# Gated mix of linear and softmax attention, one core: maxima moved to the front, and attention in cycles of two steps

## The chip, the cores and the metric

The kernel runs on one core of a Trainium2 chip. The metric is the device time of one execution in microseconds; three executions of the kernel before took 1025.98, 1026.76 and 1027.21 us (median 1026.76). A core has a matrix engine (PE, with its weight loads listed apart as PEld), a vector engine (DVE), an activation engine (ACT), a general engine (POOL), and a queue that issues DMA (SP). Each runs its own list of instructions in order, and waits on semaphores for the others.

## What is computed

The input x has 2048 rows of 448. Two attention layers with 16 heads of 28 work on it, and a gate mixes them:

```
A: q, k, v = heads(x @ A_wqkv);  pq = q @ w_phi;  pk = k @ w_phi      (per head)
   phi(p) = [softmax(p), softmax(-p)]
   o = phi_q (phi_k^T v) / (phi_q sum(phi_k) + 1e-6);   a = o @ A_wo
B: q, k, v = heads(x @ B_wqkv)
   p = softmax(q k^T * 28**-0.5);   o = p v;             b = o @ B_wo
g = sigmoid(sum(x * gate_w));   out = g a + (1 - g) b
```

## The kernel before, in words

**Order.** PE, DVE, ACT and POOL run in the order in which the Python code emits their instructions; for SP a scheduler chooses the order. So the place of a call in the source is its place in each engine's list.

**Front, about 0 to 331 us.** First come the projections of q and k of layer B (`proj_qk`, `first_units`), kept in DRAM. Then a loop over `i` (line 698) makes layer A. For its first 16 turns, `t` from 0 to 15, each turn multiplies one block of 128 rows by the folded k weights (`pk`, by `tok_major`, 11 passes, line 726) and by the v weights (`value_a`, 11 passes, line 483). Each second turn has a `proj_qk` as well, and `kv_add`. From `pk`, `features1` and `features2` make the softmax features: a copy on ACT, two reductions on DVE, two subtractions on POOL, an exponential on ACT, a sum and a reciprocal on DVE, a product on POOL. The later turns make the numerators of layer A and its output (`out_a`, tile `poa`, 12 passes) and the values of layer B (`value_b`, tile `pvb`, 11 passes). A last loop (line 878) makes `pvb` 8 to 15.

**Maxima.** The softmax of layer B subtracts the exact maximum of each row, found ahead of the scores. That work is cut into 256 units of four matmuls with 28 rows of weights each (row tiles of the array, which run at the same time). Units are made in two ways:

- In the front, `mx_unit` (line 259) writes four banks of PSUM as two tiles, `pmb` and `pmd`. ACT takes the relu of `pmd` (128x1024, line 288), two DVE operations (line 290) combine it with `pmb`. Only four banks are there for it, so the `pmd` matmuls of a unit wait for the DVE work of the unit before. `NF` = 28 units are made so: four among the last projections, one at the start of each even turn, two at turns 16 and 17, then one or two a turn from turn 24 on (lines 666, 704, 741, 787), until 28 are used up. The calls at lines 876 and 882 then find nothing left to do. Keys and queries of a unit are loaded from DRAM ahead of it (`pair_load`, `pair_query`), with two subtractions on POOL.
- In the attention loop, `mx_visit` (line 305) makes one unit in four single banks, `pm`: ACT takes the relu of one (line 326), DVE reduces the other three (lines 330 and 333), each fourth visit a further one (line 336). So 228 visits are left.

`mx_reduce` gathers the maxima of 512 rows and 4 heads (one `gq` of 16), and `load_nm` puts them, negated, into the stack of queries before the scores of that `gq` begin.

**Attention loop, about 331 to 1010 us, line 1091.** There are 16 `gq` of 16 steps, 256 steps. A step `s` makes four scores (`st`, one bank each, 128 rows of weights, line 840) and their four exponentials on ACT (`p`, line 858), the values of step `s - 1` (`pv`, column tiles of 32, line 974, eight matmuls), and a visit as long as there are visits (steps 1 to 228). So PE runs four `st`, eight `pv`, four `pm`, four `st`, and so on. Eight banks of PSUM are shared out: one for `pv`, seven for scores and visits. The lists `free`, `used` and `held` (lines 853 to 864 and 911 to 916) hand out the seven in turn; a bank can be written again when its reader, ACT or DVE, is done with it.

At the end of a `gq`, `finish` copies `pv` out on DVE (`f1`, line 399), sends the denominators through DRAM (`f2`, three steps later), multiplies on POOL (`f3`, eight steps later) and splits the product in two on POOL (`f4`). Near the end, `project` (tile `pob`, 11 passes, lines 984 and 109) makes the output of 128 rows at steps 230 to 233, 239 to 242 and 250 to 253 (`PROJ`); `load_out` fetches what it needs at the steps of `OUTS`.

Of the kernel before, what the change touches and what calls it, by code (L numbers as in the profile page):

```python
# [8 lines left out]
F32 = mybir.dt.float32  # L9
F32R = mybir.dt.float32r  # L10
# [7 lines left out]
P = 128  # L18
S = 2048
D = 448  # L20
# [3 lines left out]
NG = 4  # L24
# [2 lines left out]
SCALE = DH ** -0.5  # L27
EPS = 1e-6
NU = NG * NQ * 16
NF = 28  # L30
LOWEST = -3.0e38
OUTS = (200, 234, 243, 206)
PROJ = (230, 239, 250)


def f32(ap):
# [4 lines left out]
def gated_mix_kernel(ctx, tc, xT, wqkB, wvB, wvA, wkAT, wqAT, phi, woA, woB,  # L41
# [352 lines left out]

    def normalize1(pool, pn, nm, n):

        oU = pool.tile([P, n, 512], F32, tag="oU", name=f"oU{nm}", bufs=1 + n)
        for i in range(n):
            (nc.scalar.copy if n == 2 else nc.vector.tensor_copy)(oU[:, i, :], pn[i])
        den = pool.tile([P, n, 16], F32, tag="den", name=f"den{nm}", bufs=2)  # L400
        for i in range(n):
            nc.sync.dma_start(den[:, i, :], oU[DH:P:32, i, :])
        return oU, den

    def normalize2(pool, oU, den, nm, n, eps):

        if eps:
            nc.vector.tensor_scalar_add(den, den, EPS)
        nc.vector.reciprocal(den, den)
        rd = dr.tile([4, n * 512], F32, tag=f"rd{n}", name=f"rd{nm}", bufs=2)  # L410
        rs = pool.tile([P, n, 512], F32, tag="rs", name=f"rs{nm}", bufs=2)
        for k in range(n):
            nc.sync.dma_start(rd[:, k * 512:(k + 1) * 512], den[:, k, :])
        nc.sync.dma_start(rs.rearrange("p n q -> p (n q)"),
                          rd.unsqueeze(1).to_broadcast([4, 32, n * 512]))
        return oU, rs
# [6 lines left out]
    def normalize4(pool, oU, nm, n):  # L423

        oTn = []
        for k in range(n):
            oT = pool.tile([P, 2, 512], F32R, tag="oT", name=f"oT{nm}_{k}", bufs=2 * n)
            (nc.scalar.copy if n == 2 else nc.gpsimd.tensor_copy)(oT[:, 0, :], oU[:, k, :])
            nc.gpsimd.tensor_sub(oT[:, 1, :], oU[:, k, :], f32(oT[:, 0, :]))
            oTn.append(oT)  # L430
        return oTn
# [402 lines left out]
    def scores(s, i):  # L834

        gq, kt = divmod(s, NT)
        g, qb = divmod(gq, NQ)

        def score(j, st):
            nc.tensor.matmul(st, kst_of[(g, kt // 4)][:, j, (kt % 4) * P:(kt % 4 + 1) * P],  # L840
                             qst_of[gq][:, j, :], start=True, stop=True)
# [9 lines left out]
        sts = []  # L851
        for j in (2 * i, 2 * i + 1):
            used.append(free.pop(0))
            sts.append(bank(used[-1], f"st{s}_{j}"))
            score(j, sts[-1])
        for st in sts:
            p = late_p.tile([P, 512], F32, tag="p", name=f"p{s}_{len(pts.get(s, []))}", bufs=8)
            nc.scalar.activation(p, st, AF.Exp, scale=SCALE)  # L858
            pts.setdefault(s, []).append(p)
        if i == 1:  # L860
            a, m = used[:], held[:]
            free.extend([a[0], m[0], a[1], m[1], a[2], a[3], m[2]] if m else a)
            used.clear()
            held.clear()

    qst = [stack("qst0", False)]
    kst = [stack(f"kst{i}", True) for i in range(5)]
# [27 lines left out]

    free, used, held = list(range(7)), [], []
    spare = []

    def bank(i, nm):
# [15 lines left out]

    def spare_open():
        free.extend(held)
        held.clear()  # L920
# [90 lines left out]
    def finish(gq, s):  # L1011

        st = {}
        g, qb = divmod(gq, NQ)
        last = gq == NG * NQ - 1

        def f1():
            st["n"] = normalize1(late_p, [pv_of[gq]], f"b{gq}", 1)

        def f2():  # L1020
            st["n"] = normalize2(late_p, *st["n"], f"b{gq}", 1, False)

        def f3():
            st["n"] = normalize3(*st["n"], 1)

        def f4():
            st["o"], = normalize4(late_p, st["n"], f"b{gq}", 1)
            if g < NG - 1:
                for j in range(4):
                    r = (4 * g + j) * DH  # L1030
                    nc.sync.dma_start(o_d[r:r + DH, :, qb * 512:(qb + 1) * 512],
                                      f32(st["o"][32 * j:32 * j + DH]))

        if last:
            finish_last(gq)
            return
        f1()
        late.setdefault(s + 3, []).append(f2)
        late.setdefault(s + 8, []).append(f3)
        late.setdefault(s + 9, []).append(lambda: acts.append(f4))  # L1040
        if g == NG - 1:
            for tl in range(4):
                mids[PROJ[qb] + tl] = lambda tl=tl: project(qb, st["o"], tl)

    def finish_last(gq):

        oU = late_p.tile([P, 512], F32, tag="oU", name="oUlast", bufs=2)
        nc.vector.tensor_copy(oU, pv_of[gq])
        tail_fill(4)
        pd = bank(free.pop(0), "pd")  # L1050
# [5 lines left out]
        oT = late_p.tile([P, 2, 512], F32R, tag="oT", name="oTlast", bufs=2)  # L1056
        rw = late_p.tile([P, 16, 32], F32, tag="rs", name="rw", bufs=2)
        nc.vector.tensor_copy(rw, rc.unsqueeze(2).to_broadcast([P, 16, 32]))
        tail_fill(4)
        pr = bank(free.pop(0), "pr")  # L1060
# [27 lines left out]
            take_lows(),  # L1088
            b == 2 and nc.gpsimd.tensor_copy(woB_s[96:, 1, 2, :], woB_s[:32, 0, 2, :]))))

    for s in range(NS + 16):
        take_acts()
        if s < NS:
            gq, kt = divmod(s, NT)
            g, qb = divmod(gq, NQ)
            if s in (0, 3):
                load_k(0, 2 + s // 3)
# [6 lines left out]
            if s in OUTS:  # L1104
                load_out(OUTS.index(s))
            if g == NG - 1 and kt == 12:
                load_acc(qb)
            if s:
                scores(s, 0)
                scores(s, 1)  # L1110
        if s == NS:
            tail_open()
            tail_fill(3)
        if 0 < s <= NS:
            values(s - 1)
            if s % NT == 0:
                finish(s // NT - 1, s)
        if s:
            mx_visit()
        if mxs["f"] == len(flats):  # L1120
            mx_fin()
        if s in mids:
            mids.pop(s)()
# [4 lines left out]
        for fn in late.pop(s, []):  # L1128
            fn()


# [66 lines left out]
```

## Time and profile before

| | us |
|---|---|
| runs (three) | 1025.98, 1026.76, 1027.21 |
| the profiled execution, its own time | 1026.18 |
| span of its instructions on the core | 1024.4 |
| PE clock granted | 1.00 throughout |
| front, up to the first visits | 0 to 331 |
| 228 steps with a visit | 331 to 926 |
| 28 steps without one, with 12 projections | 926 to 1010 |
| last normalization and output | 1010 to 1024.4 |

The views of the profile used below are these. The page has busy times by engine and the chain of work that ended last. The windows give the busy time of each engine in a stretch. The timeline lists instructions in order of time, alike neighbours merged: start, length, engine, line, operation, tiles, shape, count, and in brackets the idle time before and what ended it. The chain of waits lists the pieces of the chain: start, length, what. Matmul lengths include the pipeline's latency, so what a matmul costs is read from the start of one to the start of the next.

### The profile page before, as it was taken

To read this page: it belongs to the slowest core of one execution; us is meant where nothing else is said; L and a number is where in the kernel's file an instruction comes from. 1 tells how busy PE (TensorE), PEld (TensorE's weight loads), DVE (VectorE), ACT (ScalarE), POOL (GpSimd) and SP (SyncE) were. 2 spreads that over 40 slices of the span, in tenths; PEclk is the share of its full clock that TensorE was granted. 3 is DMA by queue.
4 is the path that set the end of the run, shared out by engine and by line. 5 is a ranking of instruction groups with operands and counts; after the bars stand their busy time and mean duration, and the time that the engine had idled before them with its cause. 6 is when DMAs were issued, how large, how long until landed. Compare 5 with 4: busy or idle time off the path is not lost.

```text
span 1024.4 us, 17747 instructions
## 1 busy us (share of the span) xinstructions
PE 1014.4 (99%) x6344; PEld 560.0 (55%) x6344; DVE 685.9 (67%) x1335; ACT 811.1 (79%) x1534; POOL 244.8 (24%) x213
## 2 busy tenths in 40 slices
PE   8999999999999999999999999999999999999998
PEld 6878888878798333333333333333333333335555
DVE  5465556997610778887878878788888788882102
ACT  5354444777734999999999999999999999996672
POOL 1235456687428003301011010010120101101010
PEclk9999999999999999999999999999999999999999
DMA  8873110132337412324422223432222436312341
GB/s 295 294 245 105 51 43 22 41 90 97 97 115 153 92 47 66 82 64 107 98 53 70 72 69 84 96 70 58 70 75 64 116 95 170 85 37 78 105 126 54
DMA packets 63857, 98.65 MB, mean 96 GB/s; under 512 B 17896, under 2 KB 24664, under 8 KB 63768
## 3 DMA queue, kind: packets, MB, share of 16 engines
q1 hardware_dynamic: 63768, 97.51, 35.1%
q8 instruction: 50, 0.82, 0.4%
q14 instruction: 39, 0.32, 0.1%
HBM read 69.31 MB, written 27.78 MB: 95 GB/s over the span
## 4 chain that ended last, share of the span: by engine, by line
PE 94%; DMA 2%; DVE 2%; SPq 0%; issue 0%; ACT 0%; POOL 0%; POOLq 0%; DVEq 0%; ACTq 0%
PE st L840 28%; PE pv L974 24%; PE pm L322 10%; PE pqk L109 5%; PE poa L109 4%; PE pk L109 4%; PE pva L109 4%; PE pq L109 3%; PE pob L109 3%; PE pvb L109 2%; PE pvb L127 2%; PE pn L533 1%; PE pft L521 1%; PE pmb L285 1%; PE pkv L476 1%; PE poL L1008 1%
## 5 line engine op out<-in xcount | busy, mean ns | idle before, releaser
L858 ACT ACTIVATE p<-st 128x512 f32<-128x512 f32 x1020 | 525.8, 610 | 28.9 <-PE st L840 28.1
L333 DVE TENSOR_REDUCE part<-pm 128x1 f32<-128x512 f32 x513 | 327.6, 685 | 139.2 <-PE pm L322 132.3
L840 PE MATMUL st<-qst,kst 128*128 128x512 f32 x1024 | 316.4, 431 | 0.1
L974 PE MATMUL pv<-p,vb 128*32 128x512 f32 x2048 | 272.7, 605 | 0.0
L840 PEld LDWEIGHTS st<-qst,kst 128*128 128x128 f32 x1024 | 173.0, 187 | 130.5 <-issue 66.3
L322 PEld LDWEIGHTS pm<-kc,qc 28*128 28x128 f32 x912 | 43.6, 181 | 191.2 <-ACT p L858 182.8
L326 ACT ACTIVATE rl<-pm 128x512 f32<-128x512 f32 x228 | 136.5, 599 | 11.6
L420 POOL TENSOR_TENSOR oUb<-oUb,rsb 128x512 f32<-128x512 f32 x15 | 19.3, 1287 | 513.4 <-DMA rsb<-rdb 296.4
L330 DVE CUSTOM_DVE_ANT_0 rl<-pm,rl 128x512 f32<-128x512 f32 x171 | 116.3, 680 | 0.0
L322 PE MATMUL pm<-kc,qc 28*128 28x512 f32 x912 | 115.2, 495 | 0.0
L974 PEld LDWEIGHTS pv<-p,vb 128*32 128x32 f32 x2048 | 40.3, 108 | 65.4 <-issue 61.0
L109 PE MATMUL pqk<-XH,wB 128*128 128x512 f32 x192 | 59.6, 398 | 2.5 <-DVE ev L573 2.5
L985 DVE SCALAR_TENSOR_TENSOR acc<-pob,gate,acc 128x448 f32<-128x448 f32 x12 | 8.2, 683 | 67.9 <-PE pob L109 67.9
L572 ACT CAST ev<-pqk 128x512 fp32r<-128x512 f32 x28 | 15.9, 589 | 37.3 <-PE pqk L109 32.8
L109 PE MATMUL poa<-woA_s,oTa 128*128 128x448 f32 x192 | 42.8, 372 | 0.0
L290 DVE CUSTOM_DVE_ANT_0 rl<-pmb,rl 128x512 f32<-128x512 f32 x56 | 36.2, 684 | 8.8 <-ACT rl L288 8.8
L109 PEld LDWEIGHTS pqk<-XH,wB 128*128 128x128 f32 x192 | 35.3, 188 | 11.4 <-DVE ev L573 3.0
L573 DVE TENSOR_TENSOR ev<-pqk,ev 128x512 fp32r<-128x512 f32 x28 | 18.9, 689 | 29.7 <-ACT ev L572 29.5
L336 DVE TENSOR_REDUCE part<-rl 128x1 f32<-128x512 f32 x57 | 38.5, 675 | 0.0
L109 PEld LDWEIGHTS poa<-woA_s,oTa 128*128 128x128 f32 x192 | 35.4, 188 | 5.0 <-issue 1.8
L109 PE MATMUL pk<-wkA_s,XH 128*128 128x448 f32 x128 | 37.4, 374 | 0.0
L109 PE MATMUL pq<-wqA_s,XH 128*128 128x448 f32 x128 | 37.3, 374 | 0.0
(155 smaller groups left out, 1132.7 us busy)
## 6 DMA issues: line engine op xcount, KB each, us to landing
qkd<-ev SPq DMA_DIRECT2D x28, 512.0 KB
qst<-qkd SPq DMA_DIRECT2D x64, 224.0 KB
kst<-qkd SPq DMA_DIRECT2D x64, 224.0 KB
od<-oTb SPq DMA_DIRECT2D x48, 112.0 KB
rsa<-rda SPq DMA_DIRECT2D x8, 512.0 KB
rsb<-rdb SPq DMA_DIRECT2D x15, 256.0 KB
kc<-qkd SPq DMA_DIRECT2D x64, 56.0 KB
gad<-ga SPq DMA_DIRECT2D x16, 224.0 KB
```

The lines of the kernel that those rows point to most:

```text
L109: nc.tensor.matmul(dst, l, r, start=i == 0, stop=i == len(todo) - 1)
L127: nc.tensor.matmul(dst[:, :n], l, r, start=i == 0, stop=i == len(todo) - 1, skip_group_check=True)
L290: nc.vector.tensor_tensor_reduce(rl[:, i, :], pb[:, i, :], rl[:, i, :], 1.0, LOWEST, ALU.add, ALU.max, part[:, col + i:col + i + 1])
L322: nc.tensor.matmul(pm[j], mxs[("qc", gq)][js, qt * P:(qt + 1) * P], mxs[("kc", g, kb)][js, :], start=True, stop=True, tile_position=(32 * ...
L326: nc.scalar.activation(rl, pm[kb], AF.Relu if kb < 3 else AF.Copy)
L330: nc.vector.tensor_tensor_reduce(r, pm[j], r, 1.0, LOWEST, ALU.add, ALU.max, part[:, col + j:col + j + 1])
L333: nc.vector.tensor_reduce(part[:, col + j:col + j + 1], pm[j], AX.X, ALU.max)
L336: mxs["fin"].append(lambda: nc.vector.tensor_reduce(part[:, col + 3:col + 4], rl, AX.X, ALU.max))
L420: (nc.gpsimd if n == 1 else nc.vector).tensor_mul(oU, oU, rs)
L840: nc.tensor.matmul(st, kst_of[(g, kt // 4)][:, j, (kt % 4) * P:(kt % 4 + 1) * P], qst_of[gq][:, j, :], start=True, stop=True)
L858: nc.scalar.activation(p, st, AF.Exp, scale=SCALE)
L974: nc.tensor.matmul(pv[32 * j:32 * j + 32, :], vb[kt // 8][:, kt % 8, 4 * g + j, :], pt[j], start=kt == 0, stop=kt == NT - 1, tile_position ...
```

## The change

The attention loop takes two steps as one cycle in steps 1 to 104 and 233 to 254: eight scores, then the values of two steps (16 matmuls), then at most one visit. Steps 105 to 232 stay single, with a visit each. So 180 visits are made in the loop, 52 of them in the 52 cycles. The other 76 units are made in the front: 24 more inside the first 16 turns, at even distances within the passes of `pk` and `value_a` (`tick`, `pace`), 12 more among `poa` and `pvb` (the calls that stood there already), and 12 around and inside `pvb` 8 to 14 (the calls of lines 876 and 882). In the program, the numbers of the additional units are 5 to 7, 9 to 11 and so on up to 33 to 35, then 52 to 63, then 64 to 75.

Banks are handed out in a fixed order (`cycle_banks`): in a cycle of two steps, scores 0 to 4 take three banks of `late3` and two of `visit`, scores 5 and 7 take the banks of scores 0 and 1 again, and score 6 the third bank of `visit`. In single steps the order comes to that of before. Twelve `p` tiles are kept instead of 8; to make room, `oU`, `rs` and `oT` of the loop have one buffer instead of two. The steps of loads and projections near the end are moved, and `f3`, `f4` come a step earlier.

```
-NF = 28
+NF = 76
+LAST = 232
-OUTS = (200, 234, 243, 206)
-PROJ = (230, 239, 250)
+OUTS = (200, 238, 246, 206)
+PROJ = (234, 242, 250)
...
-        oU = pool.tile([P, n, 512], F32, tag="oU", name=f"oU{nm}", bufs=1 + n)
+        oU = pool.tile([P, n, 512], F32, tag="oU", name=f"oU{nm}", bufs=2 * n - 1)
...
-        rs = pool.tile([P, n, 512], F32, tag="rs", name=f"rs{nm}", bufs=2)
+        rs = pool.tile([P, n, 512], F32, tag="rs", name=f"rs{nm}", bufs=n)
...
-            oT = pool.tile([P, 2, 512], F32R, tag="oT", name=f"oT{nm}_{k}", bufs=2 * n)
+            oT = pool.tile([P, 2, 512], F32R, tag="oT", name=f"oT{nm}_{k}", bufs=3 * n - 2)
...
-        tok_major(pv, t, wvA_s, 450)
+        tok_major(pv, t, wvA_s, 450, tick)
...
+    pace = {}
+
+    def tick(_):
+
+        if pace["at"] and pace["n"] >= pace["at"][0]:
+            pace["at"].pop(0)
+            mx_unit()
+        pace["n"] += 1
...
         if t < NT and t % 2 == 0:
             mx_unit()
+            passes = (55 if t < NT - 4 else 44) + (4 if t >= 4 else 0)
+            pace["n"], pace["at"] = 4 if t >= 4 else 0, [k * passes // 4 for k in (1, 2, 3)]
...
-            tok_major(pk, t, wkA_s, D)
+            tok_major(pk, t, wkA_s, D, tick)
...
+        sts = [bank(b, f"st{s}_{j}") for j, b in enumerate(i)]
+        for j in range(4):
+            score(j, sts[j])
+        pts[s] = [late_p.tile([P, 512], F32, tag="p", name=f"p{s}_{j}", bufs=12) for j in range(4)]
+        for j in range(4):
+            nc.scalar.activation(pts[s][j], sts[j], AF.Exp, scale=SCALE)
...
+    late3, visit = [0, 1, 2], [3, 4, 5, 6]
+    free = []
...
+    def cycle_banks(n):
+
+        x, y = late3[:], visit[:]
+        if spare:
+            b = [(free.append(free.pop(0)), free[-1])[1] for _ in range(4 * n)]
+        elif n == 1:
+            b = x + y[:1]
+            late3[:], visit[:] = [b[2], b[3], y[3]], [b[0], y[1], b[1], y[2]]
+        else:
+            b = x + y[:2] + [x[0], y[2], x[1]]
+            late3[:], visit[:] = b[5:], [y[3], b[2], b[3], b[4]]
+        return b
+
     def mx_banks(f, first):
-        b = [free.pop(0) for _ in range(4)]
-        free.append(b[0])
-        held.extend(b[1:])
         order = [first] + sorted({0, 1, 2, 3} - {first}, key=lambda j: j == first - 1)
-        return [bank(b[order.index(j)], f"pm{f}_{j}") for j in range(4)]
+        return [bank(visit[order.index(j)], f"pm{f}_{j}") for j in range(4)]
...
-        late.setdefault(s + 8, []).append(f3)
-        late.setdefault(s + 9, []).append(lambda: acts.append(f4))
+        late.setdefault(s + 7, []).append(f3)
+        late.setdefault(s + 8, []).append(lambda: acts.append(f4))
...
-    for s in range(NS + 16):
+    first = 2 * (LAST - len(flats) // 4)
+    s = 0
+    while s < NS + 16:
+        n = 2 if 0 < s <= first or LAST < s < NS - 1 else 1
+        steps = range(s, s + n)
+        s += n
         take_acts()
...
+        if 0 < steps[0] < NS:
+            b = cycle_banks(n)
+            for i, t in enumerate(steps):
+                scores(t, b[4 * i:4 * i + 4])
...
+        for t in steps:
+            if 0 < t <= NS:
+                values(t - 1)
+                if t % NT == 0:
+                    finish(t // NT - 1, t)
+        if steps[0]:
             mx_visit()
...
```

More of the change, by code (lines that the diff above doesn't have):

```diff
@@ L850, in scores @@
             return
[L851 to L864, printed above, removed]
+        sts = [bank(b, f"st{s}_{j}") for j, b in enumerate(i)]
[4 more added lines that the diff above has]
+            nc.scalar.activation(pts[s][j], sts[j], AF.Exp, scale=SCALE)
     qst = [stack("qst0", False)]
@@ L894, in gated_mix_kernel @@
     ps2 = ctx.enter_context(tc.tile_pool(name="ps2", bufs=1, space=PSUM, reuse_waits="tile"))
-    free, used, held = list(range(7)), [], []
+    late3, visit = [0, 1, 2], [3, 4, 5, 6]
+    free = []
     spare = []
@@ L909, in gated_mix_kernel @@
             bank(i, f"first{i}")
+    def cycle_banks(n):
[9 more added lines that the diff above has]
+        return b
     def mx_banks(f, first):
-        b = [free.pop(0) for _ in range(4)]
-        free.append(b[0])
-        held.extend(b[1:])
         order = [first] + sorted({0, 1, 2, 3} - {first}, key=lambda j: j == first - 1)
-        return [bank(b[order.index(j)], f"pm{f}_{j}") for j in range(4)]
+        return [bank(visit[order.index(j)], f"pm{f}_{j}") for j in range(4)]
     def spare_open():
-        free.extend(held)
-        held.clear()
+        free.extend(late3 + visit)
         spare.append(free.pop())
@@ L1045, in finish_last @@
     def finish_last(gq):
-        oU = late_p.tile([P, 512], F32, tag="oU", name="oUlast", bufs=2)
+        oU = late_p.tile([P, 512], F32, tag="oU", name="oUlast", bufs=1)
         nc.vector.tensor_copy(oU, pv_of[gq])
@@ L1055, in finish_last @@
         nc.vector.reciprocal(rc, pd[:, :16])
-        oT = late_p.tile([P, 2, 512], F32R, tag="oT", name="oTlast", bufs=2)
-        rw = late_p.tile([P, 16, 32], F32, tag="rs", name="rw", bufs=2)
+        oT = late_p.tile([P, 2, 512], F32R, tag="oT", name="oTlast", bufs=1)
+        rw = late_p.tile([P, 16, 32], F32, tag="rs", name="rw", bufs=1)
         nc.vector.tensor_copy(rw, rc.unsqueeze(2).to_broadcast([P, 16, 32]))
@@ L1089, in gated_mix_kernel @@
             b == 2 and nc.gpsimd.tensor_copy(woB_s[96:, 1, 2, :], woB_s[:32, 0, 2, :]))))
-    for s in range(NS + 16):
+    first = 2 * (LAST - len(flats) // 4)
[4 more added lines that the diff above has]
+        s += n
         take_acts()
-        if s < NS:
-            gq, kt = divmod(s, NT)
+        for t in steps:
+            gq, kt = divmod(t, NT)
             g, qb = divmod(gq, NQ)
-            if s in (0, 3):
-                load_k(0, 2 + s // 3)
+            if t >= NS:
+                break
+            if t in (0, 3):
+                load_k(0, 2 + t // 3)
             if g + 1 < NG and qb == NQ - 1 and kt % 4 == 2:
@@ L1103, in gated_mix_kernel @@
                 load_nm(gq + 1)
-            if s in OUTS:
-                load_out(OUTS.index(s))
-            if g == NG - 1 and kt == 12:
+            if t in OUTS:
+                load_out(OUTS.index(t))
+            if g == NG - 1 and kt == (12 if qb < 2 else 14):
                 load_acc(qb)
[L1108 to L1111, printed above, removed]
+        if 0 < steps[0] < NS:
+            b = cycle_banks(n)
+            for i, t in enumerate(steps):
+                scores(t, b[4 * i:4 * i + 4])
+        if steps[0] == NS:
             tail_open()
             tail_fill(3)
[L1114 to L1118, printed above, removed]
+        for t in steps:
+            if 0 < t <= NS:
[3 more added lines that the diff above has]
+        if steps[0]:
             mx_visit()
@@ L1121, in gated_mix_kernel @@
             mx_fin()
-        if s in mids:
-            mids.pop(s)()
+        for t in steps:
+            if t in mids:
+                mids.pop(t)()
         if mxs["f"] == len(flats) and not spare:
@@ L1127, in gated_mix_kernel @@
             load_nm(NG * NQ - 1)
-        for fn in late.pop(s, []):
-            fn()
+        for t in steps:
+            for fn in late.pop(t, []):
+                fn()
 _INS = ["xT", "wqkB", "wvB", "wvA", "wkAT", "wqAT", "phi", "woA", "woB", "sel", "mask"]
```

## The prediction, made blind

> **What bounds the kernel now.** I read the page first, then the windows by stage, then the timeline of one step.
>
> ```profile
> PE 1014.4 (99%) x6344; PEld 560.0 (55%) x6344; DVE 685.9 (67%) x1335; ACT 811.1 (79%) x1534; POOL 244.8 (24%) x213
> ...
> PE 94%; DMA 2%; DVE 2%; SPq 0%; issue 0%; ACT 0%; POOL 0%; POOLq 0%; DVEq 0%; ACTq 0%
> ...
> 67.00:168.00 101.00, 101.00 (x871) 88.32 (x874) 54.83 (x104) 43.67 (x80) 57.61 (x50) 1.00 0.22 71
> 331.00:926.00 595.00, 595.00 (x3654) 233.08 (x3651) 481.45 (x970) 583.30 (x1142) 60.36 (x58) 1.00 0.34 80
> 310.00:331.00 21.00, 20.89 (x107) 17.49 (x105) 0.00 (x0) 7.83 (x14) 20.71 (x12) 1.00 0.79 170
> ```
>
> The first row is PE's share of the span, the second the share of the chain of waits; the others are stretches (PE, PEld, DVE, ACT, POOL busy, clock, DMA share, GB/s). PE is busy in all stages and makes 94% of the chain, at full clock. In the attention loop ACT is busy for 583 of 595 us too. So what counts is the time from one PE group to the next, and whether ACT or DVE hold it up. 228 steps in 595 us are 2.61 us each. One such step:
>
> ```profile
> 601.24 1.06 PE L974 MATMUL pv<-p,vb 128*32 128x512 f32 x8
> 601.69 0.61 PE L974 MATMUL pv<-p,vb 128*32 128x512 f32 x4
> 602.23 0.50 PE L322 MATMUL pm<-kc,qc 28*128 28x512 f32 x4
> 602.67 1.25 PE L840 MATMUL st<-qst,kst 128*128 128x512 f32 x4
> 603.85 1.07 PE L974 MATMUL pv<-p,vb 128*32 128x512 f32 x8
> 604.84 0.51 PE L322 MATMUL pm<-kc,qc 28*128 28x512 f32 x4
> 605.28 0.50 PE L840 MATMUL st<-qst,kst 128*128 128x512 f32 x1
> ```
>
> By starts, scores (`st`) take 603.85 - 602.67 = 1.18 us, values (`pv`) 604.84 - 603.85 = 0.99, the visit (`pm`) 602.67 - 602.23 = 0.44: together 2.61. The values come in two halves, the second 601.69 - 601.24 = 0.45 after the first, so the last half costs 0.54 with the change to the next kind of tile. What ACT, DVE and the weight loads do in that step:
>
> ```profile
> 602.77 0.60 ACT L326 ACTIVATE rl<-pm 128x512 f32<-128x512 f32 x1
> 603.26 2.06 ACT L858 ACTIVATE p<-st 128x512 f32<-128x512 f32 x4
> 602.80 1.89 DVE L333 TENSOR_REDUCE part<-pm 128x1 f32<-128x512 f32 x3 [0.72 <-PE pm L322]
> 603.42 0.19 PEld L840 LDWEIGHTS st<-qst,kst 128*128 128x128 f32 x1 [0.22 <-ACT rl L326]
> 603.85 0.16 PEld L974 LDWEIGHTS pv<-p,vb 128*32 128x32 f32 x8 [0.24 <-issue]
> ```
>
> The fourth score's weights waited for the visit's relu (`[0.22 <-ACT rl L326]`): it uses that bank again. So there is a ring: relu starts 0.54 after its `pm` and takes 0.60; 0.05 later the load starts; 0.43 after that the values; 0.99 later the next `pm`. 0.54 + 0.60 + 0.05 + 0.43 + 0.99 = 2.61, exactly the step. Steps without a visit:
>
> ```profile
> 945.02 1.20 PE L840 MATMUL st<-qst,kst 128*128 128x512 f32 x4
> 946.14 1.06 PE L974 MATMUL pv<-p,vb 128*32 128x512 f32 x8
> 947.14 1.20 PE L840 MATMUL st<-qst,kst 128*128 128x512 f32 x4
> ```
>
> Scores 1.12, values 1.00, step 2.12: here nothing waits, so in a visit step PE alone would need 1.12 + 0.99 + 0.44 = 2.55. Exponentials follow each other by (2.06 - 0.61)/3 = 0.48, the first one 0.49 after the relu.
>
> **Part 1: the cycle of two steps (52 of them with a visit).** Matmuls of one kind in a row, and units between them, are seen in pieces of the chain (start, length, what):
>
> ```profile
> 89.22 2.57 PE pqk L109 x11
> ...
> 272.47 2.65 PE poa L109 x12
> 275.56 2.43 PE pvb L109 x11
> ...
> 281.42 2.23 PE pvb L109 x11
> 283.65 2.46 PE poa L109 x12
> ```
>
> Eleven 512-wide passes in 2.57 us are 0.233 each, so eight scores take 1.12 + 4 x 0.233 = 2.05. Values of two steps take 3 x 0.45 + 0.54 = 1.90; no row shows two steps of values in a row, so the other end is 2 x 1.00 = 2.00, and I take 1.90 because the halves within a step follow at 0.45 already. With the visit, PE alone needs 2.05 + 1.90 + 0.44 = 4.39. ACT alone needs 9 x 0.48 = 4.32. The ring is longer. Score 5 takes the bank of score 0, score 7 that of score 1, and each waits for the exponential. From `pm`: relu +0.54, first exponential +0.49, second +0.48, its end +0.60, load of score 7 +0.05, values +0.43, next `pm` +1.90: 4.49. The last reducing instruction for score 6 (second of the three in 1.89 us) ends earlier than that, so DVE does not set the pace. Behind the waiting score stand the values and the visit, already in the ring.
>
> Two steps cost 5.21 to 5.22 now, so a cycle saves 0.72: 52 x 0.72 = 37.4 us. Six times in these cycles the copy of `pv` on DVE stands ahead of a visit's reductions and makes score 6 late, about 0.3 each: 1.8 us back. Single steps 105 to 232 have the same ring of banks (relu to fourth score), so 2.61 stays. Steps 229 to 232 get a visit: 4 x (2.61 - 2.12) = 1.9 lost. The 11 cycles from 233 need 2.12 + 4 x 0.233 + 0.1 for the same wait + 0.90 = 4.06, where two steps take 4.24 now: 2.0 won; their projections cost what they cost. Loop: -37.4 + 1.8 + 1.9 - 2.0 = -35.7 us.
>
> **Part 2: 48 units more in the front.** A piece `pvb` between two units took 2.43, between none 2.23; `poa` 2.65 and 2.46. So a unit among 128-row passes costs two changes, 0.20 in all, beside its 0.43 (as a `pm`): 0.63. All 48 cost 48 x 0.63 = 30.2 us, with PE full in that stage and nothing to hide them. Then the waits between units. Two units running:
>
> ```profile
> 275.06 0.50 PE L285 MATMUL pmd<-kp,qp 28*128 28x512 f32 x2
> 275.31 0.64 ACT L548 ACTIVATE ga<-poa,gate 128x448 f32<-128x448 f32 x1 [2.21 <-DMA gad<-ga]
> 275.84 1.02 ACT L288 ACTIVATE rl<-pmd 128x1024 f32<-128x1024 f32 x1
> 276.89 0.69 DVE L290 CUSTOM_DVE_ANT_0 rl<-pmb,rl 128x512 f32<-128x512 f32 x1 [1.00 <-ACT rl L288]
> 278.12 0.08 DVE L290 DVE_READ_ACCUMULATOR2_ANT part<- 128x1 f32 x1
> 278.25 0.18 PEld L285 LDWEIGHTS pmd<-kp,qp 28*128 28x128 f32 x2 [0.16 <-DVE part L290]
> ```
>
> The second unit's `pmd` waited for the first's DVE work (`[0.16 <-DVE part L290]`), 278.26 - 275.06 = 3.20 us after it; the copy `ga` stood ahead of the relu on ACT. Where nothing stands ahead the relu starts 0.54 after its `pm`, and the rest is 278.25 - 275.84 = 2.41: 2.95, about 3.0.
>
> Units 52 to 63 alternate: 0.43 + 2.65 = 3.08 after a `poa`, 0.43 + 2.43 = 2.86 after a `pvb`. Those six of 2.86 wait until 3.20: 6 x 0.34 = 2.0. Units 64 to 75 stand 7 passes apart, 0.63 + 7 x 0.20 = 2.05; there `pmd` has banks of its own that only the relu must leave (0.6 + 1.02 + 0.05 = 1.7), so no wait but 0.5 for the first. In the first 16 turns this chain of DVE work stands between units as well:
>
> ```profile
> 111.99 0.62 DVE L443 TENSOR_REDUCE extk<-pck 128x16 f32<-128x448 f32 x1 [1.53 <-ACT pck L441]
> 112.52 0.61 DVE L444 TENSOR_REDUCE extk<-pck 128x16 f32<-128x448 f32 x1
> 113.05 1.08 DVE L457 TENSOR_REDUCE fsumk<-featk 128x32 f32<-128x896 f32 x1
> 114.16 0.35 DVE L458 RECIPROCAL fsumk<-fsumk 128x32 f32<-128x32 f32 x1
> ```
>
> From 111.99 to 114.51 it takes 2.5 us, once per turn. Where it stands between two units, the second one's DVE work ends 3.0 + 2.5 + 1.3 = 6.8 after the first unit, and the third must not come sooner. Up to turn 11 units stand 14 or 15 passes apart, 3.5 to 3.7 us (two of them 7.0 to 7.4): they just pass. In turns 12 to 15 they stand 12 apart, 0.63 + 12 x 0.204 = 3.08 (two of them 6.2): three wait about 0.65, 2.0 us. Between these ends, nothing and a wait at each of the 24, I take the 2.0 as the distances say.
>
> Front: 30.2 + 2.0 + 0.5 + 2.0 = +34.7 us.
>
> **Part 3: what costs nothing, and its cover.** The loads, subtractions on POOL and SP's issues of the 48 units come earlier; DMA is busy for 0.22 in 67 to 168 us, and a unit's keys are loaded several units ahead. Behind the front POOL clears the stacks (20.7 of 21 us busy in the last window); the first visits' key differences now stand behind that. The last window grows by 8 us with its 12 units, which covers it; otherwise the first visit waits 1 to 3 us. One buffer less for `oU`, `rs`, `oT`: each is used once in 16 steps. Only POOL's write of `oT` at step 233 now waits for the projections of 237, and nothing stands behind it before 247. The chain to the last projections is on the path now (chain of waits, then timeline of PE):
>
> ```profile
> 975.81 5.73 DMA rdb<-denb
> ...
> 981.60 5.46 DMA rsb<-rdb
> ```
>
> ```profile
> 987.92 1.89 PE L109 MATMUL pob<-woB_s,oL 128*128 128x448 f32 x8
> ...
> 990.56 0.47 PE L109 MATMUL pob<-woB_s,oTb 128*128 128x448 f32 x1 [0.34 <-POOL oTb L429]
> 990.87 1.09 PE L840 MATMUL st<-qst,kst 128*128 128x512 f32 x4
> ```
>
> The denominators pass two DMAs behind the load of `oL`, then POOL, and PE's last pass waited for POOL: the projection took 990.87 - 987.92 = 2.95 where 11 passes of 0.204 and a change make 2.34. After the change that load follows the chain instead of leading it: 0.6 won. In exchange `oL` has two cycles, 8.1 us, to land; a small transfer behind it took 5.73, so I take no wait, at worst 2 us each time.
>
> **Sum.** -35.7 + 34.7 - 0.6 = -1.6 us: 1026.18 - 1.6 = 1024.6 by the profiled execution. The median of the runs stands 0.6 above it, so **1025.2**.
>
> **Rivals.** (1) *PE sets the cycle.* If scores 5 and 7 find their banks free, a cycle takes 4.39, 52 x 0.10 = 5.2 less: 1020.0. For it: ACT needs 4.32 only, and the ring has slack nowhere but there. Against: in the step of now such a wait costs exactly what the ring says. (2) *DVE paces the front.* It has 2.5 us of its own per turn, 1.3 for each unit, 0.7 for a projection: in two turns 5.0 + 5.3 + 0.7 = 11 of 15 us. If order makes each of the 36 units before `pvb` 8 wait 0.2 to 0.4 beyond my sum, it is 7 to 14 more: about 1035, slower. It decides from the point where a third unit comes within 6.8 us of the first. For it: margins of 0.2 to 0.6 us up to turn 11; against: DVE is busy for 55 of 101 us there now. The Trainium skill (TensorEngine Tiling, section "PSUM Bottleneck") says that tiling makes TensorE faster but not the evacuation of PSUM, which may then bound; by that rule this rival is the case, and the `pmd` wait above agrees with it for close units. (3) *A run of two costs two runs.* Then scores take 2.24, values 2.00, a cycle 4.68: +9.5, 1034.7, slower. Values alone would make +5, 1030. For it: no row has two steps of values in a row; against: passes of 0.233 in runs of eleven. The Trainium skill (TensorE: Matmul & The Clock Gate, section "The mechanism") says that weight loads overlap matmuls only in other row groups; by that rule scores in a row would hide no load, and this rival's time would follow. The trace differs: a load takes 0.19 (row at 603.42), and passes with a load each follow at 0.233.
>
> **Chances.** My sum holds: 0.52, with an uncertainty of 3 to 4 us around 1025.2. Rival 1: 0.20, rival 2: 0.18, rival 3: 0.10. About 0.2% (2 us) is what a measurement can tell from no change. The sum's share splits into 0.22 faster, 0.25 within, 0.05 slower; so faster 0.42, same 0.25, slower 0.33. The sum's own range is 1021 to 1029; with the rivals, 1018 to 1034 leaves out some of rival 2 and the best of rival 1.
>
> **What would show it.** From one cycle's first `st` to the next: 4.49 (rival 1: 4.39, rival 3: 4.6 to 4.7), with score 7's load waiting for ACT. Single steps of 2.61 from step 105. A `pk` or `pva` with a unit in it 0.63 longer; the chain of waits through DVE only in turns 12 to 15, and 3.2 between `pmd` among `poa` and `pvb`; first visit not waiting for POOL. The first scores should start 34.7 us later, about 361, and step 105 should begin some 36 us nearer to them. It is wrong if DVE or ACT enter the chain in the front, if a cycle is ended by a DMA, or if the last projections wait for `oL`.

## The result, and the profile after

The changed kernel takes **1033.51 us** (median of 4 runs, 1032.09 to 1033.86), the kernel before, measured beside it, 1026.37: ratio 1.0068, 95% interval 1.0051 to 1.0086. It is slower by 7.1 us, where 1.6 us less was forecast. The time lies inside the stated range, but on the other side of the kernel before. The profiled execution took 1033.35 us, with a span of 1031.6 where the kernel before had 1024.4.

On the page of the changed kernel, these two rows stand against the first two that the prediction shows of the kernel before: busy time by engine, and the chain of waits.

```profile
PE 1014.5 (98%) x6344; PEld 573.2 (56%) x6344; DVE 647.5 (63%) x1335; ACT 824.8 (80%) x1534; POOL 251.1 (24%) x218
...
PE 91%; DVE 3%; DMA 3%; POOL 1%; ACT 1%; SPq 0%; issue 0%; POOLq 0%; DVEq 0%; ACTq 0%
```

PE is busy as long as before (1014.5 and 1014.4 us), and it fell from 99 to 98%. So the loss is not work of PE; it is time in which PE waited or, as will be seen, ran slowly. Its share of the chain fell from 94 to 91%. The waits of PE from the first scores to the end name the places (in us: total, count, longest):

```profile
PE st L852 <- DMA qst<-nm: 4.6, 1, 4.6
PE pob L110 <- DVE acc L1000: 2.3, 3, 0.8
PE st L852 <- ACT rl L327: 0.7, 1, 0.7
PE pm L323 <- POOL kc L197: 0.6, 1, 0.6
PE st L852 <- ACT p L860: 0.3, 1, 0.3
```

The first is at step 64, the second at three pairs of projections, the third at the first score of step 128 (the profile names the relu, but the score that takes the relu's bank is the fourth), the fourth at the visit of step 107, and the last at step 1, whose first score waited for the exponentials of step 0.

The kernel before had one wait there between steps 1 and 255, the 0.3 that the prediction quotes. To set sizes, the span is cut at the starts of the first score matmul of some steps (us; "forecast" is the prediction's difference):

| stretch | before | after | difference | forecast |
|---|---|---|---|---|
| start to first score (step 0) | 326.51 | 360.17 | +33.7 | +34.7 |
| step 0 to 1 | 2.44 | 2.82 | +0.4 | 0 |
| steps 1 to 105: cycles of two | 271.12 | 240.07 | -31.1 | -35.6 |
| steps 105 to 229: single | 323.23 | 325.14 | +1.9 | 0 |
| steps 229 to 255 | 82.66 | 84.98 | +2.3 | -0.7 |
| step 255 to end | 18.44 | 18.39 | 0 | 0 |

The differences add up to the 7.2 us between the spans. (The first 67 us, the same work in all kernels here, end between 65.95 and 68.78 in the profiled executions, at 66.85 before and 67.56 after; so 0.7 of the first row is noise.)

**One usual cycle** (timeline of the changed kernel):

```profile
375.88 0.51 PE L323 MATMUL pm<-kc,qc 28*128 28x512 f32 x4
376.31 2.23 PE L852 MATMUL st<-qst,kst 128*128 128x512 f32 x8
376.41 0.60 ACT L327 ACTIVATE rl<-pm 128x512 f32<-128x512 f32 x1
376.91 4.02 ACT L868 ACTIVATE p<-st 128x512 f32<-128x512 f32 x8
...
378.47 1.92 PE L989 MATMUL pv<-p,vb 128*32 128x512 f32 x16
380.32 0.51 PE L323 MATMUL pm<-kc,qc 28*128 28x512 f32 x4
```

From `pm` to `pm` it is 380.32 - 375.88 = 4.44; the median of the 52 cycles is 4.45, where 4.49 was forecast. Scores take 378.47 - 376.31 = 2.16, values 380.32 - 378.47 = 1.85, the visit 0.43. So the values of two steps are 0.05 shorter than forecast, and the ring with 1.855 for them (0.54 + 0.49 + 0.48 + 0.60 + 0.05 + 0.43 + 1.855 = 4.445) is the measured cycle.

**One cycle is not usual.** That of steps 63 and 64 took 11.51 us. PE there, and the granted clock (the column ahead of the DMA share) in stretches of 2 us (two of them left out):

```profile
501.40 0.51 PE L323 MATMUL pm<-kc,qc 28*128 28x512 f32 x4
501.84 1.25 PE L852 MATMUL st<-qst,kst 128*128 128x512 f32 x4
507.73 2.05 PE L852 MATMUL st<-qst,kst 128*128 128x512 f32 x4 [4.64 <-DMA qst<-nm]
509.71 3.27 PE L989 MATMUL pv<-p,vb 128*32 128x512 f32 x16
512.91 0.51 PE L323 MATMUL pm<-kc,qc 28*128 28x512 f32 x4
```

```profile
504.00:506.00 2.00, 0.00 (x0) 0.00 (x0) 0.00 (x0) 0.50 (x2) 0.00 (x0) 0.91 0.96 184
...
510.00:512.00 2.00, 2.00 (x12) 0.39 (x8) 0.00 (x0) 0.67 (x2) 0.00 (x0) 0.50 0.08 14
512.00:514.00 2.00, 2.00 (x15) 0.68 (x7) 0.82 (x2) 0.56 (x2) 0.00 (x0) 0.88 0.00 0
```

The scores of step 64, the first of a new group of heads, waited 4.64 us for its queries (`qst`) and maxima (`nm`). After that wait the clock was 0.50, and the same values took 512.91 - 509.71 = 3.20 instead of 1.85. Wait and slow clock together cost 11.51 - 4.45 = 7.06 us. That this is as much as the whole result is chance: without it the other gains and losses would have left the kernel about level with the one before.

**Why they came late** is in SP's list of DMA issues, of the kernel before (first) and of the changed one (second):

```profile
454.57 0.63 SPq L402 DMA_DIRECT2D denb<-oUb  x1
...
466.20 0.92 SPq L814 DMA_DIRECT2D kst<-qkd  x2
476.10 3.41 SPq L1031 DMA_DIRECT2D od<-oTb  x4
...
482.41 2.89 SPq L826 DMA_DIRECT2D qst<-nm  x4
```

```profile
471.00 0.60 SPq L403 DMA_DIRECT2D denb<-oUb  x1
...
483.96 1.69 SPq L826 DMA_DIRECT2D kst<-qkd  x2
492.93 3.75 SPq L1046 DMA_DIRECT2D od<-oTb  x4
...
499.52 2.47 SPq L838 DMA_DIRECT2D qst<-nm  x4
```

In both, SP stands still for 7 to 9 us ahead of the store `od`, which needs POOL's `oTb`, the end of the chain of the denominators (`denb`, `rdb`, `rsb`, POOL). Behind it stand the loads for step 64. (`kst` are keys, `qst` the stack of queries and maxima; in the rows left out three blocks of keys and three of queries stand between `od` and the maxima.) From `denb` to `od` the chain takes 492.93 - 471.00 = 21.9 us after and 476.10 - 454.57 = 21.5 before. That is 8.2 steps of 2.61 us, but 9.8 of 2.23. From `od` to step 64's scores there were 493.19 - 476.10 = 17.1 us before; after, they would have been due at 502.92 (1.08 behind 501.84, as in the cycles around), 10.0 us behind `od`, and they came after 507.73 - 492.93 = 14.8. So the kernel before had some 2.3 us to spare, if its loads took as long, and faster steps took 17.1 - 10.0 = 7.1 of the distance.

### The profile page after: what moved, and what is told of

It reads as the page before. It is cut to its first block, busy times and chain, and to the rows that moved or that the text cites. A ratio compares the mean times of both kernels' runs of the same rounds, so it can differ in the third digit from the quotient of the medians.

```text
span 1031.6 us, 17673 instructions
## 1 busy us (share of the span) xinstructions
PE 1014.5 (98%) x6344; PEld 573.2 (56%) x6344; DVE 647.5 (63%) x1335; ACT 824.8 (80%) x1534; POOL 251.1 (24%) x218
## 4 chain that ended last, share of the span: by engine, by line
PE 91%; DVE 3%; DMA 3%; POOL 1%; ACT 1%; SPq 0%; issue 0%; POOLq 0%; DVEq 0%; ACTq 0%
PE st L852 27%; PE pv L989 23%; PE pm L323 7%; PE pqk L110 5%; PE poa L110 4%; PE pk L128 4%; PE pva L128 3%; PE pmb L286 3%; PE pob L110 3%; PE pq L110 2%; PE pvb L110 2%; PE pvb L128 2%; PE pn L534 1%; PE pqk L636 1%; DMA kst<-qkd 1%; PE pft L522 1%
## 5 line engine op out<-in xcount | busy, mean ns | idle before, releaser
L334 DVE TENSOR_REDUCE part<-pm 128x1 f32<-128x512 f32 x405 | 258.8, 686 | 172.7 <-PE pm L323 168.5
L852 PE MATMUL st<-qst,kst 128*128 128x512 f32 x1024 | 304.7, 428 | 5.6 <-DMA qst<-nm 4.6
L989 PE MATMUL pv<-p,vb 128*32 128x512 f32 x2048 | 261.1, 605 | 0.0
L421 POOL TENSOR_TENSOR oUb<-oUb,rsb 128x512 f32<-128x512 f32 x15 | 19.4, 1291 | 505.6 <-DMA rsb<-rdb 310.8
L291 DVE CUSTOM_DVE_ANT_0 rl<-pmb,rl 128x512 f32<-128x512 f32 x152 | 98.3, 684 | 58.1 <-ACT rl L289 58.0
L327 ACT ACTIVATE rl<-pm 128x512 f32<-128x512 f32 x180 | 107.6, 598 | 11.6 <-PE pm L323 4.5
L289 ACT ACTIVATE rl<-pmd 128x1024 f32<-128x1024 f32 x76 | 78.1, 1028 | 38.2 <-PE pmd L286 31.0
L331 DVE CUSTOM_DVE_ANT_0 rl<-pm,rl 128x512 f32<-128x512 f32 x135 | 92.0, 681 | 0.0
L323 PE MATMUL pm<-kc,qc 28*128 28x512 f32 x720 | 91.3, 495 | 0.6 <-POOL kc L197 0.6
L286 PE MATMUL pmd<-kp,qp 28*128 28x512 f32 x152 | 38.0, 496 | 0.7 <-DVE part L291 0.7
L128 PE MATMUL pva<-wvA_s,XH 128*128 128x450 f32 x128 | 37.9, 372 | 0.0
```

Source lines behind the costliest of these rows:

```text
L286: nc.tensor.matmul((pb if j < 2 else pd)[:, j % 2, :], qc[js, qt * P:(qt + 1) * P], kc[js, :], start=True, stop=True, tile_position=(32 * ...
L289: nc.scalar.activation(rl, pd, AF.Relu)
L291: nc.vector.tensor_tensor_reduce(rl[:, i, :], pb[:, i, :], rl[:, i, :], 1.0, LOWEST, ALU.add, ALU.max, part[:, col + i:col + i + 1])
L323: nc.tensor.matmul(pm[j], mxs[("qc", gq)][js, qt * P:(qt + 1) * P], mxs[("kc", g, kb)][js, :], start=True, stop=True, tile_position=(32 * ...
L327: nc.scalar.activation(rl, pm[kb], AF.Relu if kb < 3 else AF.Copy)
L331: nc.vector.tensor_tensor_reduce(r, pm[j], r, 1.0, LOWEST, ALU.add, ALU.max, part[:, col + j:col + j + 1])
```

## Experiments

All are edits of the changed kernel. The theory (1): the loss is work that stands behind the chain of the denominators on an in-order list, plus one bank that two projections share. The rivals are in the expectations.

**e1, e2, e3.** e1 asks for queries and maxima of step 64 four steps sooner:

```
-            if kt == 12 and gq + 1 < NG * NQ:
+            if kt == (8 if gq == 3 else 12) and gq + 1 < NG * NQ:
                 load_q(gq + 1)
-            if kt == (12 if gq + 1 < 14 else 14) and gq + 1 < NG * NQ - 1:
+            if kt == (8 if gq == 3 else 12 if gq + 1 < 14 else 14) and gq + 1 < NG * NQ - 1:
                 load_nm(gq + 1)
```

e2 puts the first projection of a late cycle ahead of its values:

```
+        if len(steps) == 2 and steps[0] in mids:
+            mids.pop(steps[0])()
         for t in steps:
             if 0 < t <= NS:
                 values(t - 1)
```

e3 has both.

> The loads of the queries and maxima for step 64 are issued with step 56 instead of step 60, ahead of the store that waits on SyncE for POOL. Theory 1 (the 7 us of the cycle at step 63 are one late transfer, held up in SyncE's order, and the slow clock after it): cycle 63 takes 4.7 instead of 11.5, the mean clock of the attention stage is back at 1.00, and the time falls by 6.8 us to about 1026.7. Rival (the transfers are late because the DMA engines are full in that stretch, whatever the order): the stall moves or shrinks to 1 to 3 us, time 1028 to 1031. Rival (the slow clock is an accident of the chip and not a result of the wait): it stays, with 2 us or more of the loss.

> In a late cycle with two projections the first is put between the scores and the values, so that VectorE has 1.85 us to empty their one bank. Theory 1 (each pair of projections loses 0.95 us on that bank): three pairs, 2.8 us less, about 1030.7, no wait of pob for VectorE. Rival (the late cycles lose on ScalarE or on the rotation of six banks, the wait for VectorE only takes the place of that one): less than 1 us changes, 1032.5 to 1033.5.

> Both edits. If the two losses are separate they add up: 1033.5 - 6.8 - 2.8 = 1023.9, faster than the kernel before (1026.4) by 2.5 us. If one hides the other, it ends above 1025.

| kernel | us, median | ratio to before, 95% interval | steps 1 to 105 | 105 to 229 | 229 to 255 |
|---|---|---|---|---|---|
| before | 1026.37 | 1 | 271.12 | 323.23 | 82.66 |
| the change | 1033.51 | 1.0068 (1.0051 to 1.0086) | 240.07 | 325.14 | 84.98 |
| e1 | 1026.93 | 1.0010 (1.0000 to 1.0020) | 233.03 | 327.88 | 85.71 |
| e2 | 1031.49 | 1.0047 (1.0031 to 1.0063) | 241.33 | 325.37 | 82.18 |
| e3 | 1024.21 | 0.9983 (0.9973 to 0.9993) | 233.00 | 326.91 | 82.63 |

Each ratio is to the kernel before as measured beside that run, 1026.04 us for e1 to e4.

In e1 cycle 63 takes 4.57 us, and steps 1 to 105 fall by 7.0: the stall is gone with its slow clock. In e2 the late stretch falls by 2.8. Together they end 0.17% below the kernel before. Theory 1 holds for both, and the slow clock was no accident of its own. e2 ended 0.8 above its forecast; in its profiled execution cycle 63 took 12.92, 1.4 more than in the change. But e1 and e3 still lose 3.7 to 4.6 us in the single steps, more than the change itself, so something was left: in e1 steps 127 to 129 take 4.88, 3.34 and 3.26 instead of 2.61, a wait of 2.2 us for keys at step 128 and a slow clock behind it (last section), and step 107 takes 3.73. What these steps wait for comes below.

The wait that e2 removes, in the changed kernel (timeline):

```profile
950.86 0.78 PE L110 MATMUL pob<-woB_s,oTb 128*128 128x448 f32 x3
951.68 0.68 DVE L1000 SCALAR_TENSOR_TENSOR acc<-pob,gate,acc 128x448 f32<-128x448 f32 x1 [5.58 <-PE pob L110]
952.42 1.89 PE L110 MATMUL pob<-woB_s,oL 128*128 128x448 f32 x8 [0.78 <-DVE acc L1000]
```

The second projection writes the bank that DVE has to empty first; both stand in one cycle now, where a step stood between them before.

**e4** changes the order of banks in a cycle with a visit:

```
-            b = x + y[:2] + [x[0], y[2], x[1]]
+            b = x + y[:2] + [x[1], y[2], x[0]]
```

> In the cycles of two steps with a visit, scores 5 and 7 change their banks: score 5 takes that of score 1, score 7 that of score 0. Theory 1 (a ring from the visit over relu, the exponential of score 1 and the score that takes its bank sets the cycle): the wait comes two scores earlier, 2 x 0.23 = 0.46 more per cycle, 4.91 instead of 4.45, 52 x 0.46 = 24 us: about 1057. Rival (TensorE or ScalarE by their own work set the cycle): 4.45 stays, 1033.5. The transfer for step 64 then has more time, which may give back up to 7 us.

Measured 1049.61 us, where 1057 less up to 7 was expected (ratio 1.0226, 1.0212 to 1.0240). The median cycle is 4.91 us, as the ring said. Steps 1 to 105 took 258.42 us, 18.4 more than in the change: 51 cycles at 0.46 are 23.5, cycle 63 took 8.13 and so 3.4 less, and what eight other cycles of the change have above 4.45 (1.9 us, mostly copies of `pv`) is hidden in the longer cycle: 23.5 - 3.4 - 1.9 = 18.2. The rival falls. The single steps took 323.09, so the 1.9 us that the change loses there are gone too. Its cycle (timeline of e4):

```profile
377.37 0.51 PE L323 MATMUL pm<-kc,qc 28*128 28x512 f32 x4
377.81 1.47 PE L852 MATMUL st<-qst,kst 128*128 128x512 f32 x5
377.90 0.60 ACT L327 ACTIVATE rl<-pm 128x512 f32<-128x512 f32 x1 [0.39 <-PE pm L323]
...
379.53 0.96 PE L852 MATMUL st<-qst,kst 128*128 128x512 f32 x3 [0.25 <-ACT p L868]
380.43 1.92 PE L989 MATMUL pv<-p,vb 128*32 128x512 f32 x16
```

Now score 5 waits for the second exponential, 379.53 - 377.37 = 2.16 us after the visit, and three scores and the values still follow. ACT is idle ahead of the relu (0.39), so neither ACT nor PE by its own work sets this cycle.

**e5 and e7** leave the loads of step 64 at their step and change what stands ahead of them: e5 the store (with POOL's copy and subtraction ahead of it, which `f4` holds as well), e7 a block of keys.

```
-        late.setdefault(s + 8, []).append(lambda: acts.append(f4))
+        late.setdefault(s + (12 if gq == 2 else 8), []).append(lambda: acts.append(f4))
```

```
-            if g + 1 < NG and qb == NQ - 1 and kt % 4 == 2:
-                load_k(g + 1, kt // 4)
+            if g + 1 < NG and qb == NQ - 1 and (kt % 4 == 2 and t != 58 or t == 61):
+                load_k(g + 1, 2 if t == 61 else kt // 4)
```

> Loads stay where the change has them; only the store of the third block of outputs (od, which waits on SyncE until POOL has made oTb) is moved from step 57 to step 61, behind the loads for step 64. Theory 1 (SyncE holds the loads behind that wait): the loads are issued some 5 us sooner, cycle 63 takes 4.6 to 5 and not 11.5, the time is about 1026.7. Rival (the bytes of queries and keys take too long for ten steps of 2.22 us, with no part for the store): cycle 63 stays above 8, and the time above 1030.

> The store stays where the change has it, with its wait. One block of four key transfers (0.9 MB, first needed at step 72) goes from ahead of the queries and maxima of step 64 to behind them. If what the queue holds ahead counts as much as the wait: at 207 GB/s the block takes 4.3 us of the 4.6 that the score waited, so cycle 63 takes 4.6 to 5.2 and the clock stays at 1.00; about 1027. If the wait on SyncE alone counts: only the 1.4 us in which the block is issued are won, cycle 63 takes 8 to 10, 1030 to 1032.

e5 took 1027.01 us (1.0016, 1.0005 to 1.0028) with 4.55 for cycle 63, e7 1027.13 (1.0017, 1.0005 to 1.0028) with 4.75; like e1 they still lose 3.2 to 5.1 us in the single steps. SP's list in e5:

```profile
485.07 3.02 SPq L826 DMA_DIRECT2D kst<-qkd  x5
488.46 3.53 SPq L826 DMA_DIRECT2D qst<-qkd  x3
492.49 4.21 SPq L838 DMA_DIRECT2D qst<-nm  x4
497.31 3.88 SPq L1046 DMA_DIRECT2D od<-oTb  x4
```

SP doesn't stand still now. Either edit alone is enough: the stall needs both, the hold behind the store and a full queue of transfers behind it. The rival of e5 (bytes alone) falls, and so does that of e7 (the hold alone, 8 to 10 us).

**e8, e10 and e9.** e8 moves the chain's end later for the first three groups of heads (POOL's multiplication `f3` and the step `f4`) and has e2's edit; e10 moves `f4` alone and has e2's edit.

```
-        late.setdefault(s + 7, []).append(f3)
-        late.setdefault(s + 8, []).append(lambda: acts.append(f4))
+        late.setdefault(s + (10 if g < NG - 1 else 7), []).append(f3)
+        late.setdefault(s + (12 if g < NG - 1 else 8), []).append(lambda: acts.append(f4))
```

e9 is one part alone: `NF = 28`, `LAST = 228`, no units from `tick`, and e2's edit.

> Outputs of the first three groups: POOL's multiplication three steps later, the store four steps later, each time; and the first of two projections ahead of the values. Theory 1 (the waits at steps 64, 107 and 128 are all the same thing: work that stands on SyncE or POOL behind the chain of the denominators, which takes as long as before while the steps have become shorter or the visits' loads have moved): no wait at any of them; 1033.5 - 6.8 - 2.6 - 1.9 = 1022.2. Rival (the waits at 107 and 128 have other causes, the visits' rows being late by themselves): 1024, as with the other two edits together.

> As the run with the chain late, but POOL's multiplication stays where the change has it; only the store is moved for the first three groups. Theory 1 (at step 128 the loads stand behind the store on SyncE, at step 107 the visit's key difference stands behind the multiplication on POOL): the wait at 128 goes, that of 1.0 us at 107 stays; 1021.5, 1 us above the run with the chain late. Rival (both waits come from the store): no wait at either, 1020.6.

> One part alone: the front with 28 units as before, all of steps 1 to 228 single with a visit each, and cycles of two only from step 229, with the first of two projections ahead of the values. If the account of the trace is right, the late cycles win 0.2 us each, 2 to 3 us in all: 1023.5 to 1024.5; and what moving 48 visits and joining 104 steps is worth without any stall is the difference to the run with the chain late, about 2 us or less. If the late cycles win nothing, 1026.4.

| kernel | us, median | ratio to before, 95% interval | steps 1 to 105 | 105 to 229 | 229 to 255 |
|---|---|---|---|---|---|
| e8 | 1020.57 | 0.9954 (0.9941 to 0.9967) | 232.97 | 323.41 | 82.37 |
| e10 | 1021.25 | 0.9948 (0.9930 to 0.9967) | 233.06 | 323.03 | 82.07 |
| e9 | 1023.87 | 0.9985 (0.9976 to 0.9994) | 271.35 | 323.49 | 80.83 |

e8 and e10 are the fastest (their intervals overlap). e8 is 4.7 us below the kernel before as measured beside it (1025.32; 1026.52 beside e10), and all its single steps are back at 2.61. Against the change its stretches lose 7.1, 1.7 and 2.6 us, 11.4 where 11.3 was forecast; of the 1.5 that are left to 1020.57 the kernel before, measured beside it, took 1.05 less too. Its waits of PE from the first scores on, all of them:

```profile
PE st L852 <- ACT p L860: 0.3, 1, 0.3
PE pob L110 <- DMA oL<-od: 0.2, 1, 0.2
```

So the waits at steps 107 and 128 were of the same kind. e10 was forecast to keep that of step 107, and it didn't (its step 107 takes 2.66). No wait at either step is what its rival had, but for step 107 it was not the store alone: `f4` holds POOL's copy and subtraction as well. POOL in the changed kernel (first) and in e10 (second):

```profile
606.41 1.28 POOL L421 TENSOR_TENSOR oUb<-oUb,rsb 128x512 f32<-128x512 f32 x1 [12.79 <-DMA rsb<-rdb]
607.76 0.61 POOL L429 CAST oTb<-oUb 128x512 fp32r<-128x512 f32 x1
608.45 1.29 POOL L430 TENSOR_TENSOR oTb<-oUb,oTb 128x512 fp32r<-128x512 f32 x1
609.82 1.27 POOL L197 TENSOR_TENSOR kc<-kc,kd 28x512 fp32r<-28x512 f32 x1
```

```profile
600.62 1.30 POOL L421 TENSOR_TENSOR oUb<-oUb,rsb 128x512 f32<-128x512 f32 x1 [13.77 <-DMA rsb<-rdb]
602.00 1.29 POOL L197 TENSOR_TENSOR kc<-kc,kd 28x512 fp32r<-28x512 f32 x1
```

A visit's keys (`kc`) stood behind the whole chain on POOL, ready at 611.09; in e10 they are ready at 603.29, before their visit at 603.58. The kernel before made these visits four steps sooner, so its keys came ahead of the chain. For step 128 SP's list of the changed kernel has these rows behind the store, which is issued at 646.68:

```profile
650.13 1.69 SPq L826 DMA_DIRECT2D kst<-qkd  x3
651.88 1.69 SPq L177 DMA_DIRECT2D qc<-qkd  x4
653.61 3.19 SPq L826 DMA_DIRECT2D qst<-qkd  x4
656.91 2.55 SPq L838 DMA_DIRECT2D qst<-nm  x4
```

Seven blocks of keys and queries (224 KB each) and a visit's four loads (`qc`) stand ahead of the maxima there; in the kernel before it was four blocks, and the rest had been issued ahead of the store. e4 leaves the store where it was and has seven blocks and no `qc` behind it: its step 127 takes 2.69. e1 has eight blocks and one `qc`, and waits 2.2 us. So by the lists it is here too the store's hold together with the loads behind it; no run took the store apart from POOL's two operations.

e9 shows that late cycles alone (13 of them) win 82.66 - 80.83 = 1.8 us, a little less than the 2 to 3 expected. e8 has 11 of them, so moving 48 visits and joining 104 steps is worth about 1023.87 - 1020.57 = 3.3 us without stalls, more than the 2 or less expected.

**e6** undoes the late cycles (`n = 2 if 0 < s <= first else 1`).

> The change with the cycles of two after step 232 undone: single steps there, one projection each. Theory 1 (late cycles win about 2 us and lose 2.8 to the bank of two projections): 0 to 1 us less than the change, 1032.7 to 1033.5, and from step 229 to 255 84.2 to 85.0 us. Rival (late cycles are worth their 2 us as built, the loss is elsewhere): 1035.5.

Measured 1032.05 us (ratio 1.0056, 1.0036 to 1.0077), 0.7 below the range that was expected; steps 229 to 255 took 84.00, 0.2 below it and 1.0 less than in the change. The rival falls. So as built the late cycles lost 1.0 against single steps, and with e2's edit they win 84.00 - 82.18 = 1.8.

## Why the prediction was wrong

- **The cycle: right.** The ring set it (4.45 for 4.49), and e4 moved it by the amount that the ring gives. Rival 1 (PE sets the cycle, 4.39) falls; so does rival 3: eight scores without a wait take 2.06 (954.76 to 956.82 in a late cycle) and not 2.24, values 1.85. The rule that weight loads overlap matmuls only in other row groups (the Trainium skill, TensorE: Matmul & The Clock Gate, section "The mechanism", which also allows a background weight buffer) was no reason for that rival: if no load were hidden, a score would cost its load of 0.19 beside its 0.23, and eight some 3.4. The trace differs from it here too. Without the stall the cycles win 271.12 - 232.97 = 38.2 us, 2.5 more than the sum had: the values of two steps are 0.05 shorter in each cycle.
- **The front: right.** +33.7 for +34.7. By stages, from the starts of the same passes: the 24 units in the 16 turns cost 16.8 (first `pk` to first `pq`; forecast 17.1), the 12 among `poa` and `pvb` 8.5 (last `pq` to `pvb` 8; 9.6), the last 12 6.6 (to the first score; 8.1). Another 1.1 was lost among the `pq` passes, where the sum had nothing, and 0.7 is noise of the first 67 us. Rival 2 (DVE paces the front) falls; PE waited for DVE between 67 and 360 us three times, 0.7 us in all:

```profile
PE pmd L286 <- DVE part L291: 0.7, 3, 0.3
```

- **Copies of `pv` in the cycles: right** (1.6 for 1.8 in the six cycles behind a copy; cycles 15 and 47 have 0.3 more).
- **Part 3, "what costs nothing", failed**, and it decides the result. It tested the denominators' chain only at the last projections, and DMA only by its mean share in the front. The chain's length stayed at 22 us while the steps in it became shorter, so what waits behind it in SP's list came 1.6 steps later, more than the margin at step 64 held: +7.1 us, of which 4.6 is the wait and 2.4 the clock after it. The rows of the kernel before could have told it: 17.1 us from the store to step 64, about 10 after the change, of which issuing the store and the loads takes 9.2 (476.10 to 485.30). How long the loads themselves take, 14.8 from the store on, only the changed kernel's trace gives. The prediction named "a cycle is ended by a DMA" as what would make it wrong, and didn't price it.
- **"So 2.61 stays" for single steps failed by 1.9 us.** Banks were the same, but visits come four steps later there, and their key differences met the chain on POOL at step 107, and at step 128 more loads than before stand behind the store on SP's list.
- **"Their projections cost what they cost" failed by 2.8 us.** Two in a cycle share one bank, three times 0.95.
- Beside these, 0.4 us between steps 0 and 1, of which 0.3 is the wait for the exponentials of step 0. The misses: +7.1 + 1.9 + 2.8 + 0.4 - 2.5 (cycles) - 1.0 (front) = 8.7, the distance from -1.6 to +7.2 but for 0.1.
- **That the time lies inside the stated range is luck.** The range went up to 1034 for rivals 2 and 3, and neither is what happened; the sum's own range ended at 1029.

## What to carry to other kernels

When steps get shorter, list every chain of fixed length (DMA there and back, a slow engine) and count in new steps when its result comes; then look at what stands behind its last instruction on each in-order list, SP's above all. A mean DMA share says nothing of that: here it was the loads of one cycle of 52. And where two uses of one buffer move into one cycle, the buffer's emptying is a wait.

## What the runs showed of the hardware

A wait of PE can cost more than itself. In the wait of 4.64 us the granted clock fell to 0.50 (by the share 0.91 at about 505.6, 2.6 us after the last score at 503.1), until about 512.5, and 16 value matmuls took 3.20 instead of 1.85 us. In e1 a shorter gap did the same; PE there, and the clock:

```profile
654.95 0.51 PE L323 MATMUL pm<-kc,qc 28*128 28x512 f32 x4
657.66 1.15 PE L852 MATMUL st<-qst,kst 128*128 128x512 f32 x4 [2.20 <-DMA kst<-qkd]
658.74 1.60 PE L989 MATMUL pv<-p,vb 128*32 128x512 f32 x8
```

```profile
658.00:660.00 2.00, 2.00 (x12) 0.50 (x10) 0.00 (x0) 1.84 (x4) 0.00 (x0) 0.78 0.36 83
660.00:662.00 2.00, 2.00 (x10) 1.12 (x7) 1.55 (x3) 1.00 (x3) 0.00 (x0) 0.50 0.00 0
662.00:664.00 2.00, 2.00 (x15) 0.67 (x13) 1.02 (x3) 1.89 (x4) 0.00 (x0) 0.86 0.29 65
```

After 2.2 us the next matmuls began at full clock; by the shares 0.78 and 0.86 the clock fell to 0.50 at about 659.1, 1.5 us after the first of them, and was back at 1.00 at about 662.6. The Trainium skill (TensorE: Matmul & The Clock Gate, section "Part 1: The HAM clock gate") says that the clock halves after an idle window of about 3.4 us. Both differ from it here: in the long wait the clock fell after 2.6 us, and the gap of 2.2 us is shorter than that window; the measurement decides. The length of the gap alone does not tell what follows: 1.48 us without a matmul in e3 were followed by 0.50 too, 1.39 us in e7 were not, and in the front 2.55 us in the kernel before and 3.41 us in e2 left the clock at 1.00. What else decides is not shown. Waits of 0.8 us (at `pob`) left the clock at 1.00.
